# First three projection units made together, their inputs fetched in another order, two warming passes fewer

## The chip, the cores and the metric

The kernel runs on one core of one Trainium2 chip. The metric is the device time of one execution in microseconds (us), taken as the median of several runs. A core has a matrix engine (PE, with PEld as its weight loads), three elementwise engines (DVE, ACT, POOL), and a queue engine (SP) that issues transfers. ACT and POOL can issue transfers as well. Each engine works through its own list of instructions in order and waits on counters (semaphores) that other engines or transfers raise.

## The reference

Two branches over the same input `x` (2048 tokens by 448) are mixed by a gate:

```python
g = sigmoid((x * gate_w).sum(-1, keepdims=True))
q, k, v = split(x @ wqkv)                 # 16 heads of 28
a = softmax(q @ k.T * 28 ** -0.5) @ v     # per head
a = a.reshape(1, 2048, 448) @ wo
gate = x @ W_gate; gate = gate * (gate > 0)
b = (gate * (x @ W_up)) @ W_down          # inner width 1792
out = g * a + (1 - g) * b
```

All inputs and outputs are float32. The kernel keeps that accuracy by cutting operands into two parts: a *high* part, the value rounded to the PE's `float32r` type, and a *low* part, the rest. A product is then the sum of high times high, low times high and high times low.

## The kernel before, in words

The work has three stages: the projections q, k, v and the gate's sums from `x`; attention with the gate and up products mixed in; and the output and down products. Only the start of the first stage changes.

**Tiles.** The 448 rows of `x` and of the weights are cut into four chunks of 128 partitions (the last holds 64 rows twice). The tokens are cut into four blocks of 512 (`tb`). A unit `qk(tb, c)` makes 128 columns of q or k (`c` from 0 to 6) for one block: 11 matmuls of 128x512, listed in `TERMS`, that add up in one PSUM bank. A term `(a, b)` multiplies part `a` of the weights `W` (0 to 2 high of chunks 0 to 2, 3 to 5 their low, 6 the fourth chunk) with part `b` of the tokens `X` (0 to 3 high, 4 to 7 low). Four banks go round for these units.

**Getting the operands.** `load_x(tb)` fetches a block of `x` into staging tiles `xr` (three of them go round, each holds two chunks), `load_w(c)` fetches 224 columns of the weights. `split_first`, `split_x` and `split_w` cut what arrived: `act_high` (line 130, ACT) makes the high part, `low` (line 136, DVE) or `pool_low` (line 139, POOL) subtracts it to make the low one. 224 columns (2*GD) are one group, so unit 0 needs the first group, unit 2 the second, and unit 1 both.

**Order.** The engines' order is the order of the code (a manual schedule). `split_first` takes the first group's four chunks and the tokens' four chunks in this order:

```python
for group in ((weights(0), tokens(0)), (weights(1), tokens(1)), (weights(2), weights(3)),
              (tokens(2), tokens(3))):
```

Then the second group of weights is split (`split_w(*w1)`), and the units follow: (0,0) with its terms by chunk (`BY_CHUNK`), (0,1), (1,0), (1,1), (0,2), (2,0), (2,1), (1,2), (3,0), and from there the list `mixed`, in which units, v products (`vproj`) and the first maxima of the scores (`smax`, line 191) alternate. The scores' maxima begin with unit number 20, counted from the first.

**Before the first unit** PE makes `WARM` passes (line 398): matmuls of zeros, 128x512, whose result is overwritten.

**After a unit** `send()` makes a high and a low copy of its bank (ACT, then DVE), and POOL stores both to DRAM (`qk_d`, line 359). When the four units (0..3, 0) are stored, SP loads from there the K and Q of the first heads (`load_k`, `load_q`, lines 175 and 180).

**Transfers.** Loads are issued by SP (the first two pieces of weights by ACT). Eight counters, DMAHW0 to DMAHW7, are given to these loads in turn: the ninth load has to wait until the first has landed, since it uses the same counter. An `xr` tile can be filled again when DVE has read it.

Of the kernel before, what the change touches and what calls it, by code (L numbers as in the profile page):

```python
# [18 lines left out]
P = 128  # L19
# [17 lines left out]
WARM = 11  # L37
# [41 lines left out]
def gated_mix_kernel(ctx, tc, x, wq, wo, wgu, wd, out):  # L79
# [156 lines left out]
    with tc.tile_pool(name="qkv", bufs=1) as pa:  # L236
        W = pa.tile([P, 7, WC], F32R, name="W")

        def load_w(c):
            c0, c1 = c * 2 * GD, (c + 1) * 2 * GD if c < G + 1 else 2 * D + VC  # L240

            if c in (0, 2, 5):
# [5 lines left out]
            if c > 0:  # L248
                nc.sync.dma_start(wr, wq[:, :, c0:c1])
            return wr, c0, c1  # L250

        def split_w(wr, c0, c1):

            ways = [[(W[:, :, c0:c1], wr)]]
            if c0 < 2 * D:
# [4 lines left out]
                if c0 == 2 * GD:  # L260
                    ways = [[(w[:, :, :, 0], r[:, :, :, 0])], [(w[:, :, a, 1:], r[:, :, a, 1:]) for a in range(2)]]
# [8 lines left out]
        def split_first(wr, xr):  # L270

            r = wr.rearrange("p c (a j d) -> p c a j d", a=2, j=4)
            w = W[:, :, :2 * GD].rearrange("p c (j a d) -> p c a j d", a=2, j=4)

            def weights(c):
                act_high(w[:, c if c < 3 else 6], r[:, c])
                yield

                take = pool_low if c else low
                if c < 3:  # L280
                    take(w[:, 3 + c], r[:, c], w[:, c])
                else:
                    take(w[64:, 6], r[64:, 3], w[64:, 6])
                yield
# [8 lines left out]
            for group in ((weights(0), tokens(0)), (weights(1), tokens(1)), (weights(2), weights(3)),  # L293
                          (tokens(2), tokens(3))):
# [4 lines left out]
        def load_x(tb):  # L299
            r = []  # L300
            for c in range(0, 4, 2):
                xr = pa.tile([P, 2, TB], F32, name=f"xr_{tb}_{c}", tag="stg", bufs=3)
                for a, b in ((c, c + 1), (c + 1, c + 2)) if tb == 0 else ((c, c + 2),):
                    nc.sync.dma_start(xr[:, a - c:b - c], x[:, a:b, tb * TB:(tb + 1) * TB])  # L304
                if tb + c == 0:
                    load_first(nc.sync, 2, 4)
# [42 lines left out]
        def qk(tb, c, terms=TERMS, among=()):  # L349
            ps = ps_any(c == NQ - 1)  # L350
            for n, (a, b) in enumerate(terms):
                nc.tensor.matmul(ps, W[:, a, c * P:(c + 1) * P], xf(tb, b), start=(n == 0), stop=(n == NT - 1))  # L352
                mix(n, among)
            st = st_tile(tb, c)
# [54 lines left out]
        split_first(w0[0], x0)  # L409
# [4 lines left out]
        split_w(*w1)  # L414
        qk(0, 0, BY_CHUNK)
        split_x(1, x1)

# [22 lines left out]
        units = [(qk, 3, 1), (qk, 2, 2), (qk, 3, 2)]  # L440
        units += [(qk, tb, c) for c in range(3, NQ) for tb in range(NB - 1, -1, -1)]
        vs = [(vproj, tb, t) for tb in range(NB - 1, -1, -1) for t in range(4)]
        mixed = units[:2]
# [447 lines left out]
```

## Time and profile before

| what | value |
|---|---|
| median of 3 runs | 1260.32 us (1259.86 to 1260.8) |
| profiled execution: first to last instruction (span) | 1258.2 us |
| median of the runs less that span | 2.1 us |
| PE busy in the span | 1252.8 us of 1258.2 |
| DVE, ACT, POOL busy | 854.8, 748.4, 374.3 us |
| granted PE clock, mean | 1.000 |

The profile shows one execution, and of it only the time from its first to its last instruction; about 2.1 us of a run's time lie outside. A row of the timeline gives a start, a duration, the engine, the line, the operation with its output and input, and in brackets how long the engine was idle before it and what ended that. "us, mean ns" of a group are its total and the mean of one instruction.

### The profile page before, as it was taken

The page shows a single profiled execution, that of the slowest core. Times are in us where ns is not written, and L with a number is a line of the kernel's source. Part 1 is how long each engine was busy: PE and PEld are TensorE (multiplying, and loading weights), DVE is VectorE, ACT ScalarE, POOL GpSimd, SP SyncE. Part 2 cuts the span into 40 slices and gives each one's busy share as a digit, 9 for nine tenths or more (in the row PEclk, how much of TensorE's full clock was granted, in tenths as well). Part 3 has the DMA queues.
Part 4 walks back from the last instruction along what each step waited for, and adds up shares of the span by engine and source line. Part 5 has one row for each costly group of instructions (what it writes and reads, how often), then busy time and mean ns, then how long its engine had stood idle before and what let it go on. Part 6 is the DMA issues. An engine that isn't in the chain of part 4 may idle for free.

```text
span 1258.2 us, 18270 instructions
## 1 busy us (share of the span) xinstructions
PE 1252.8 (100%) x6687; PEld 919.1 (73%) x6687; DVE 854.8 (68%) x1363; ACT 748.4 (59%) x1424; POOL 374.3 (30%) x569
## 2 busy tenths in 40 slices
PE   9999999999999999999999999999999999999998
PEld 6888866677666676666766667766667666899997
DVE  6599767687777797776977778877778224663342
ACT  6312767686666776666866667766677773312121
POOL 4222222312334123423133331134222444651020
PEclk9999999999999999999999999999999999999999
DMA  8955453144245314241544323142431226634432
GB/s 302 315 206 209 117 155 99 50 106 104 60 115 173 81 43 121 68 113 44 130 121 127 100 80 90 43 122 67 114 94 50 84 85 208 223 110 138 145 106 79
DMA packets 54113, 151.00 MB, mean 120 GB/s; under 512 B 10304, under 2 KB 17416, under 8 KB 49160
## 3 DMA queue, kind: packets, MB, share of 16 engines
q1 hardware_dynamic: 36632, 100.44, 29.2%
q0 software_dynamic: 16960, 48.94, 11.0%
q8 instruction: 52, 0.85, 0.3%
q10 hardware_dynamic: 432, 0.46, 0.1%
q14 instruction: 37, 0.30, 0.1%
HBM read 104.16 MB, written 46.03 MB: 119 GB/s over the span
## 4 chain that ended last, share of the span: by engine, by line
PE 99%; DMA 0%; SPq 0%; DVE 0%; ACT 0%; issue 0%
PE b L526 22%; PE b L191 19%; PE b L217 19%; PE b L560 18%; PE b L789 11%; PE b L352 5%; PE b L370 3%; PE b L744 3%; DMA xr<-x 0%; PE b L199 0%; SPq L304 0%; DVE X L136 0%; DVE y L795 0%; ACT X L130 0%; SPq L384 0%
## 5 line engine op out<-in xcount | busy, mean ns | idle before, releaser
L192 DVE TENSOR_REDUCE mx<-b 128x1 f32<-128x512 f32 x1024 | 646.5, 685 | 51.2 <-PE b L191 50.7
L219 ACT ACTIVATE P<-b 128x512 f32<-128x512 f32 x840 | 467.1, 599 | 160.8 <-PE b L217 139.0
L526 PE MATMUL b<-X,wg 128*128 128x512 f32 (+1 forms) x1232 | 415.3, 394 | 0.0
L191 PE MATMUL b<-K,Q 128*128 128x512 f32 x1024 | 389.6, 391 | 0.0
L217 PE MATMUL b<-Q,K 128*128 128x512 f32 x1024 | 389.3, 390 | 0.0
L526 PEld LDWEIGHTS b<-X,wg 128*128 128x128 f32 (+1 forms) x1232 | 220.2, 187 | 53.8 <-issue 9.3
L217 PEld LDWEIGHTS b<-Q,K 128*128 128x128 f32 x1024 | 192.3, 188 | 46.3 <-issue 6.7
L191 PEld LDWEIGHTS b<-K,Q 128*128 128x128 f32 x1024 | 192.4, 188 | 44.3 <-issue 5.9
L560 PE MATMUL b<-P,V 128*32 128x512 f32 x1680 | 188.2, 593 | 0.0
L548 POOL DMA_DIRECT2D h_d<-h x56 | 31.3, 558 | 405.4 <-DVE h L542 354.9
L139 POOL TENSOR_TENSOR wg<-wgr,wg 128x384 fp32r<-128x384 f32 x200 | 143.2, 731 | 10.4 <-DVE wg L133 2.0
L560 PEld LDWEIGHTS b<-P,V 128*32 128x32 f32 x1680 | 52.7, 110 | 120.0 <-issue 116.8
L789 PE MATMUL b<-WD,hh 128*128 128x448 f32 x672 | 138.5, 365 | 0.0
L219 ACT ACTIVATE V<-b 128x512 f32<-128x512 f32 x184 | 105.0, 599 | 48.8 <-PE b L217 42.3
L789 PEld LDWEIGHTS b<-WD,hh 128*128 128x128 f32 x672 | 126.2, 188 | 10.3
L130 ACT ACTIVATE hh<-hr 128x512 fp32r<-128x512 f32 x56 | 35.3, 631 | 124.7 <-PE b L789 120.2
L136 DVE TENSOR_TENSOR hh<-hr,hh 128x512 fp32r<-128x512 f32 x56 | 45.7, 815 | 66.4 <-ACT hh L130 66.3
L352 PE MATMUL b<-X,W 128*128 128x512 f32 x308 | 83.1, 393 | 0.1
L566 DVE TENSOR_TENSOR os<-b,os 128x512 f32<-128x512 f32 x16 | 11.1, 692 | 86.5 <-PE b L560 86.5
L352 PEld LDWEIGHTS b<-X,W 128*128 128x128 f32 x308 | 57.4, 188 | 14.5 <-DVE X L136 1.6
L130 ACT ACTIVATE wg<-wgr 128x384 fp32r<-128x384 f32 x156 | 62.2, 490 | 7.9 <-DMA wgr<-wgu 3.9
L575 POOL DMA_DIRECT2D l_d<-rs x16 | 8.9, 559 | 186.2 <-DVE rs L574 186.2
(74 smaller groups left out, 665.6 us busy)
## 6 DMA issues: line engine op xcount, KB each, us to landing
wgr<-wgu SPq DMA_DIRECT2D x55, 512.0 KB
K<-qk_d SPq DMA_DIRECT2D x64, 224.0 KB
Q<-qk_d SPq DMA_DIRECT2D x64, 224.0 KB
h_d<-h POOLq DMA_DIRECT2D x56, 256.0 KB, 2.7
hr<-h_d SPq DMA_DIRECT2D x56, 256.0 KB
qk_d<-st POOLq DMA_DIRECT2D x21, 512.0 KB, 4.2
x_d<-X POOLq DMA_DIRECT2D x6, 1024.0 KB, 5.4
X<-x_d SPq DMA_DIRECT2D x24, 256.0 KB
```

The costliest lines, as they stand in the source:

```text
L130: nc.scalar.activation(dst, src, AF.Copy)
L136: nc.vector.tensor_tensor(dst, src, f32(high), op=OP.subtract)
L139: nc.gpsimd.tensor_tensor(dst, src, f32(high), op=OP.subtract)
L191: nc.tensor.matmul(ps, Q[h][:, u * P:(u + 1) * P], K[h % 3][:, c * TB:(c + 1) * TB], start=True, stop=True)
L192: nc.vector.tensor_reduce(MX[h][:, 4 * u + c:4 * u + c + 1], ps, axis=AX.X, op=OP.max)
L217: nc.tensor.matmul(ps, K[h % 3][:, kt * P:(kt + 1) * P], Q[h][:, j * TB:(j + 1) * TB], start=True, stop=True)
L219: nc.scalar.activation(PT[i][:, j], ps, AF.Exp, scale=SCALE)
L352: nc.tensor.matmul(ps, W[:, a, c * P:(c + 1) * P], xf(tb, b), start=(n == 0), stop=(n == NT - 1))
L370: nc.tensor.matmul(ps[:, :VC], xf(tb, b)[:, t * P:(t + 1) * P], W[:, a, 2 * D:2 * D + VC], start=(n == 0), stop=(n == NT - 1))
L526: nc.tensor.matmul(ps, WS[i][rows, s, a], xf(i // NF, b)[rows], start=(n == 0), stop=(n == NT - 1))
L560: nc.tensor.matmul(po[32 * j:32 * j + 32], V[:, h // 4 % 2, i % NK, h % 4], p[:, j], start=(i == i0), stop=(i == i0 + ni - 1))
L789: nc.tensor.matmul(ACC[i // NF][t][:, :D], HH[i][:, a, t * P:(t + 1) * P], WD[:, f, b], start=(f == 0 and n == 0), stop=(f == NF - 1 and n ...
```

## The change

- The second group of weights is no longer fetched and split as a whole (`load_w(1)`, `split_w(*w1)` are gone); both groups come chunk by chunk with the tokens, chunk 0 first. The first pieces, chunk 0 of the tokens and chunk 0 of the first group, are fetched in two halves of 64 partitions, one on SP's queue and one on ACT's.
- `split_first` goes by chunk: tokens, first group, second group. For chunk 0 the first group's high part is made by DVE (`dve_high`, line 133). The lows of the first group are made by DVE, those of the second by POOL.
- Units (0,0), (0,1) and (0,2) are made together by `qk_first`: three banks, and for each chunk all terms of all three units, before the next chunk. Their copies and stores come after all 33 matmuls.
- `WARM` is 9 and not 11.
- `split_x(1)` stands ahead of the units. The order of the units is now these three, then (1,0), (1,1), (1,2), (2,0), (2,1), (2,2), (3,0): the fourth block's first unit is the tenth, where it was the ninth. From the twelfth unit on, the order is as before, and the numbers that count units in `mixed` are one lower.

```diff
-WARM = 11
+WARM = 9
...
-            if c in (0, 2, 5):
+            if c == 5:
...
-            if c > 0:
-                nc.sync.dma_start(wr, wq[:, :, c0:c1])
+            nc.sync.dma_start(wr, wq[:, :, c0:c1])
...
-            def weights(c):
-                act_high(w[:, c if c < 3 else 6], r[:, c])
+            def weights(g, c):
+                r = wr[:, c, 2 * GD * g:2 * GD * (g + 1)].rearrange("p (a j d) -> p a j d", a=2, j=4)
+                w = W[:, :, 2 * GD * g:2 * GD * (g + 1)].rearrange("p c (j a d) -> p c a j d", a=2, j=4)
+                (act_high if c + g else dve_high)(w[:, c if c < 3 else 6], r)
                 yield
-                take = pool_low if c else low
+                take = pool_low if g else low
...
-            for group in ((weights(0), tokens(0)), (weights(1), tokens(1)), (weights(2), weights(3)),
-                          (tokens(2), tokens(3))):
+            for c in range(4):
+                group = [tokens(c), weights(0, c), weights(1, c)]
                 for _ in range(2):
...
-                    nc.sync.dma_start(xr[:, a - c:b - c], x[:, a:b, tb * TB:(tb + 1) * TB])
-                if tb + c == 0:
-                    load_first(nc.sync, 2, 4)
+                    if tb + a == 0:
+                        for queue, rows in ((nc.sync, slice(0, 64)), (nc.scalar, slice(64, P))):
+                            queue.dma_start(xr[rows, :1], x[rows, :1, :TB])
+                            load_first(queue, 0, 0, 1, rows)
+                    else:
+                        nc.sync.dma_start(xr[:, a - c:b - c], x[:, a:b, tb * TB:(tb + 1) * TB])
+                    if tb == 0:
+                        load_first(nc.sync, a, a == 0, 2)
...
+        def qk_first():
+            units = [(c, ps_any()) for c in range(3)]
+            for c in range(4):
+                terms = [t for t in TERMS if t[1] % 4 == c]
+                order = [(t, u) for t in terms for u in units]
+                if c == 0:
+                    order = [(terms[n], units[k]) for n, k in ((0, 0), (1, 0), (0, 1), (0, 2), (2, 0), (2, 1), (2, 2), (1, 1), (1, 2))]
+                for (a, b), (u, ps) in order:
+                    nc.tensor.matmul(ps, W[:, a, u * P:(u + 1) * P], xf(0, b), start=b == 0 and a == 0,
+                                     stop=(a, b) == terms[-1] and c == 3)
+            for u, ps in units:
+                send_qk(0, u, ps)
...
+            send_qk(tb, c, ps)
+
+        def send_qk(tb, c, ps):
             st = st_tile(tb, c)
...
-        w0 = load_w(0)
-
-        def load_first(queue, a, b):
-            queue.dma_start(w0[0][:, a:b], wq[:, a:b, w0[1]:w0[2]])
-
-        for c in range(2):
-            load_first(nc.scalar, c, c + 1)
+        def load_first(queue, c, a, b, rows=slice(0, P)):
+            queue.dma_start(w0[rows, c, a * 2 * GD:b * 2 * GD], wq[rows, c, a * 2 * GD:b * 2 * GD])
+
         x0 = load_x(0)
-        w1 = load_w(1)
...
-        split_w(*w1)
-        qk(0, 0, BY_CHUNK)
         split_x(1, x1)
+        qk_first()
...
-        qk(0, 1, HIGH_FIRST)
+        qk(1, 0)
         split_x(2, x2)
         x3 = load_x(3)
-        qk(1, 0)
+        qk(1, 1)
         split_w(*w2)
-        qk(1, 1)
-        qk(0, 2)
+        qk(1, 2)
         split_x(3, x3)
...
-        qk(1, 2)
-        qk(3, 0)
         split_w(*w4)
         w3 = load_w(3)
+        qk(2, 2)
+        qk(3, 0)
```

How the change moves instructions is shown at three places. A row is a line of the code, an operation, its output and input, the output's size, and in brackets the counters that it, or a bare wait standing directly ahead of it, waits for; X_105 is the high part of the first block of tokens, X_106 the low part, V the buffer in which the first weights land. The first place is the head of ACT's list, from its two transfers to the first pieces it splits, before:

```order
L384 DMA V<-wq 128x224 x2
L130 ACT_TABLE_LOAD
L130 ACTIVATE W<-V 128x2x4x28 [waits DMAHW0_49]
L130 ACTIVATE X_105<-xr_0_127 128x512 [waits DMAHW1_49]
L130 ACTIVATE W<-V 128x2x4x28 [waits DMAHW2_49]
L130 ACTIVATE X_105<-xr_0_127 128x512 [waits DMAHW3_49]
```

and with the change, where DMAHW0 counts ACT's half of the first tokens and DMAHW1 SP's half:

```order
L302 DMA xr_0_125<-x 64x512
L402 DMA V<-wq 64x224
L130 ACT_TABLE_LOAD [waits DMAHW1_49]
L130 ACTIVATE X_105<-xr_0_125 128x512 [waits DMAHW0_49]
L130 ACTIVATE W<-V 128x2x4x28 [waits DMAHW4_49]
L130 ACTIVATE X_105<-xr_0_125 128x512 [waits DMAHW5_49]
L130 ACTIVATE W<-V 128x2x4x28 [waits DMAHW6_49]
```

The tokens moved ahead of the weights, and the first ACTIVATE needs two transfers; the wait for one of them is a bare wait that stands ahead of the table load. The second place is PE after its warming passes, before (the first unit alone, bank b_69):

```order
L352 MATMUL b_69<-X_105,W 128x512 [waits Activation_49]
L352 MATMUL b_69<-X_105,W 128x512 [waits DVE_49]
L352 MATMUL b_69<-X_106,W 128x512 [waits DVE_49]
L352 MATMUL b_69<-X_105,W 128x512 [waits Activation_49]
L352 MATMUL b_69<-X_105,W 128x512 [waits Pool_49]
```

and with the change (three banks, b_69, b_70 and b_73):

```order
L366 MATMUL b_69<-X_105,W 128x512 [waits DVE_49,Activation_49]
L366 MATMUL b_69<-X_105,W 128x512 [waits DVE_49]
L366 MATMUL b_70<-X_105,W 128x512 [waits Activation_49]
L366 MATMUL b_73<-X_105,W 128x512
L366 MATMUL b_69<-X_106,W 128x512
L366 MATMUL b_70<-X_106,W 128x512
L366 MATMUL b_73<-X_106,W 128x512
L366 MATMUL b_70<-X_105,W 128x512 [waits Pool_49]
L366 MATMUL b_73<-X_105,W 128x512
```

Chunk 0 now has nine matmuls where it had three; the second in the list still needs DVE, for the low part of the first weights. The third place is DVE between its clearing of the warming operand and the end of the first chunk, before:

```order
L394 MEMSET V 128x256
L136 TENSOR_TENSOR W<-V,W 128x2x4x28 [waits DMAHW0_49,Activation_49]
L136 TENSOR_TENSOR X_106<-xr_0_127,X_105 128x512 [waits DMAHW1_49,Activation_49]
L136 TENSOR_TENSOR X_106<-xr_0_127,X_105 128x512 [waits DMAHW3_49,Activation_49]
L136 TENSOR_TENSOR X_106<-xr_2_131,X_105 128x512 [waits DMAHW5_49,Activation_49]
```

and with the change:

```order
L409 MEMSET V 128x256
L133 CAST W<-V 128x2x4x28 [waits DMAHW3_49,DMAHW2_49]
L136 TENSOR_TENSOR X_106<-xr_0_125,X_105 128x512 [waits DMAHW1_49,DMAHW0_49,Activation_49]
L136 TENSOR_TENSOR W<-V,W 128x2x4x28 [waits DVE_49]
L136 TENSOR_TENSOR X_106<-xr_0_125,X_105 128x512 [waits DMAHW5_49,Activation_49]
```

The copy of the first weights came to DVE, and the low part of these weights, which stood first, now stands behind the low part of the tokens.

More of the change, by code (lines that the diff above doesn't have):

```diff
@@ L447, in gated_mix_kernel @@
             units, vs = units[2:], vs[2:]
-        spills = {15 + 3 * k: (NB - 1 - k // 2, k % 2) for k in range(6)}
-        m, first, ahead = 0, 10, 4 * LEAD + 16
+        spills = {14 + 3 * k: (NB - 1 - k // 2, k % 2) for k in range(6)}
+        m, first, ahead = 0, 9, 4 * LEAD + 16
         for n, (f, *a) in enumerate(mixed):
```

23 lines of the change are left out of this document (10 added, 13 removed).

## The prediction

> **What bounds the kernel now.** I read the page's head first, then the chain that ended last, then busy time by stretch, and only then the first 16 us instruction by instruction.
>
> ```profile
> span 1258.2 us, 18270 instructions
> PE 1252.8 (100%) x6687; PEld 919.1 (73%) x6687; DVE 854.8 (68%) x1363; ACT 748.4 (59%) x1424; POOL 374.3 (30%) x569
> PE 99%; DMA 0%; SPq 0%; DVE 0%; ACT 0%; issue 0%
> 0.00:100.00 100.00, 98.66 (x430) 80.09 (x431) 70.65 (x113) 35.12 (x76) 30.42 (x49) 1.00 0.75 262
> 1200.00:1258.20 58.20, 54.10 (x267) 49.78 (x266) 20.82 (x29) 11.07 (x17) 5.22 (x6) 0.99 0.30 91
> ```
>
> The matrix engine is the bound nearly everywhere: it is on the chain for 99%, idle for 1.34 us in the first 100 us and for 4.10 us in the last 58. The change touches only the start, so what can be had lies there. The chain's first pieces and PE's weight loads show it. In the latter, the bracket names what ended each idle time.
>
> ```profile
> 2.64 4.97 DMA xr<-x
> ...
> 8.30 0.99 DVE X L136
> ...
> 9.33 30.44 PE b L352 x133
> ```
>
> ```profile
> 1.20 4.09 PE L398 MATMUL b<-V 128*128 128x512 bf16 x11 [1.20 <-DVE V L394]
> ...
> 3.73 0.15 PEld L398 LDWEIGHTS <-V 128*128 128x128 bf16 x1 [0.28 <-issue]
> 4.16 0.15 PEld L398 LDWEIGHTS <-V 128*128 128x128 bf16 x1 [0.28 <-issue]
> 4.49 0.31 PEld L398 LDWEIGHTS <-V 128*128 128x128 bf16 x2 [0.17 <-issue]
> 5.37 0.30 PEld L352 LDWEIGHTS b<-X,W 128*128 128x128 f32 x2 [0.57 <-ACT X L130]
> 6.10 0.62 PEld L352 LDWEIGHTS b<-X,W 128*128 128x128 f32 x3 [0.43 <-DVE X L136]
> ...
> 9.33 0.75 PEld L352 LDWEIGHTS b<-X,W 128*128 128x128 f32 x4 [0.36 <-DVE X L136]
> ```
>
> From 9.33 us PE runs without a stop. The 133 matmuls from there take 30.44 us, 0.229 us each, and a unit of 11 takes 2.52. They end with unit 13, 143 matmuls in all, so 10 were done before 9.33. From 5.37 to 9.33 that is 3.96 us for 2.29 us of work: 1.67 us lost while chunks arrive and are split. Between the warming passes, weight loads start 0.43 us apart up to 4.16 and less after it: PE was at about half speed until some 4.3 us, 3.1 us after its first pass.
>
> My yardstick is the end of the 33rd matmul, when units 1 to 3 are done in both kernels. Before: 9.33 + 23 x 0.229 = 14.60 us.
>
> **The change, part by part.** *More work per chunk.* Nine matmuls of chunk 0 are 2.06 us where three were 0.69, more than a chunk takes to split (below). So once chunk 0 is complete, PE no longer waits for the next. That removes the 1.67 us of stalls. What it does to the start depends on the next step.
>
> *The table load.* ACT's first operation needs its table, and the trace has its price:
>
> ```profile
> 1.67 1.28 ACT L130 ACT_TABLE_LOAD   x1 [1.67 <-PEq L884]
> 4.41 0.39 ACT L130 ACTIVATE W<-V 128x224 fp32r<-128x224 f32 x1 [1.46 <-DMA V<-wq]
> 4.71 0.61 ACT L130 ACTIVATE X<-xr 128x512 fp32r<-128x512 f32 x1
> ...
> 4.41 0.39 SPq L304 DMA_DIRECT2D xr<-x  x1
> ...
> 4.83 0.39 DVE L136 TENSOR_TENSOR W<-V,W 128x224 fp32r<-128x224 f32 x1 [3.69 <-ACT W L130]
> 5.35 0.69 DVE L136 TENSOR_TENSOR X<-xr,X 128x512 fp32r<-128x512 f32 x1
> ```
>
> Before, it ran from 1.67 to 2.95, hidden by the wait for data until 4.41. With the change a bare wait for SP's half of the tokens stands ahead of it in ACT's list, so the 1.28 us start when that half lands. No row shows this 128 KB load. The nearest is ACT's first weight piece of 112 KB, issued at the same moment: SP's load that has to wait for its counter goes at 4.41, so it had landed by then. From above, the 256 KB of chunk 0 were there by 4.71. From below, the page's quickest transfer of such size bounds it:
>
> ```profile
> h_d<-h POOLq DMA_DIRECT2D x56, 256.0 KB, 2.7
> L133 DVE CAST wg<-wgr 128x384 fp32r<-128x384 f32 x6 | 1.9, 358 | 0.1
> L139 POOL TENSOR_TENSOR W<-V,W 128x224 fp32r<-128x224 f32 x2 | 1.5, 750 | 3.4 <-ACT W L130 3.4
> L139 POOL TENSOR_TENSOR W<-V,W 64x224 fp32r<-64x224 f32 x1 | 1.1, 1082 | 0.1
> ```
>
> that is 0.75 (the first issue) + 2.7 = 3.45. I take 4.41, the row of the same size and moment. Then: table load to 5.69; high part of the tokens (0.61) to 6.32; PE's first matmul at 6.36, 0.99 later than before; low part of the tokens (DVE, 0.69) to 7.03; low part of the first weights (0.39), now behind it, to 7.42. PE's second matmul waits for that: 7.46. The copy that went to DVE (under 0.36) runs during the table load and costs nothing. From the second matmul, 32 in a row end at 7.46 + 32 x 0.229 = 14.79.
>
> *Is that row unbroken?* ACT needs 0.61 + 2 x 0.39 = 1.39 us per chunk; DVE 0.69 + 0.39 = 1.08; POOL 0.75 to 1.08; PE uses 2.06. ACT reaches the chunks' tokens at 6.7, 8.0 and 9.4, PE needs chunk 1 at 9.3, chunk 2 at 11.4, chunk 3 at 13.4. The loads have about as much cover:
>
> ```profile
> 6.93 1.33 ACT L130 ACTIVATE X<-xr 128x512 fp32r<-128x512 f32 x2
> 8.94 1.42 ACT L130 ACTIVATE W<-wr 128x168 fp32r<-128x168 f32 x6 [0.67 <-DMA wr<-wq]
> ```
>
> Tokens and both weight groups, 1.9 MB, were in by 8.94 before. The bytes are the same, but three of SP's issues (weights 2, tokens 3, weights 3) now wait for counters that come free when the first halves land, so they go after 4.41; even 1.5 us on 8.94 is before ACT's use at 10.4 could hurt PE at 13.4. The block `split_x(1)` follows on ACT at 10.8 and ends, with DVE's lows, near 14.5; unit 4 needs its first high part at 14.8.
>
> *Two warming passes fewer.* The nine end at about 4.7 (the tenth's weights load at 4.49 as the ninth starts). Nothing for PE is ready before 6.36, so this neither gains nor costs, as long as the clock stays up.
>
> *The order of the units* costs PE nothing in itself: units 12 and on follow as before. The fourth block's tokens are needed after nine units and not eight, so this wait gets 2.52 us more room.
>
> *Sum:* 14.79 - 14.60 = +0.19 us on a span of 1258.2. The median of the runs stands 2.1 us above that span, and I put the change on it: 1260.32 + 0.19 = 1260.5. With the landing at 3.45 or 4.71 the sum is -0.77 or +0.49.
>
> **Rivals.** *The clock falls back (slower).* PE now idles from 4.7 to 6.36, does one matmul, and idles until 7.46: 1.66 and 0.87 us of idling within 2.8. For it: the half-speed start above shows that the clock follows activity, and the two spare passes are gone. Against it: stalls of up to 0.57 us in this trace left the pace at 0.229. If it falls back just then, regaining it takes the 3.1 us seen, half of them lost: +0.19 + 1.55 = +1.7; if the regaining is missed once, +0.19 + 3.1 = +3.3. It decides if the stop before the second matmul is long enough. The Trainium skill, "TensorE: Matmul & The Clock Gate" (Part 1, the HAM clock gate) puts the window at about 3.4 us, free-running, and wants one idle window for the fall; by that rule, stops of 1.66 and 0.87 us leave the clock up, and the sum stays as it is. The 3.1 us of slow passes agree with its figure.
>
> *The table load has a tail (slower).* Before, ACT idled 1.46 us behind it and a transfer ended that, so a hidden tail of up to 1.46 us would not have shown. Exposed now, it moves both matmuls: +0.19 + 1.46 = +1.65, and PE would then idle from 4.7 to 7.8 in one piece, which makes the first rival likely on top: +3.2 to +4.8. Against it: the profile shows no instruction there. The Trainium skill, "ScalarE: Activation LUTs" (What ACT_TABLE_LOAD costs) gives 1283 ns, as this trace does, and a drain of about 1380 ns with each switch of tables; by that page the sum would be +1.57. No run here shows a drain.
>
> *The table load goes ahead (faster).* If it runs at 1.67 as before, the high part of the tokens ends at 5.02, both lows at 6.12, and 33 matmuls at 6.15 + 32 x 0.229 = 13.48: -1.1; with data at 3.45, some -2.1. The list of ACT speaks against it.
>
> *The wait goes elsewhere (slower).* The last first-column unit (3,0) is tenth now. Before, its store let head 0's loads go at 38.15; their last was in by 52.76, when SP could reuse its counter; the first maxima needed it at 54.27.
>
> ```profile
> 38.15 1.52 SPq L175 DMA_DIRECT2D K<-qk_d  x2
> ...
> 52.76 0.31 SPq L180 DMA_DIRECT2D Q<-qk_d  x1
> ...
> 54.27 0.39 PE L191 MATMUL b<-K,Q 128*128 128x512 f32 x1
> ...
> 8.79 3.56 POOL L411 MEMSET K<- 32x2048 f32 x2
> ```
>
> That is 1.51 us of room against one unit, 2.52: up to +1.0, and +1.2 with the sum. POOL's clearing of K, 3.56 us, now stands behind its last low part at about 11.7 instead of at 8.79, so the first stores go some 3 us later; if none of that is caught up, about +3. Against it: one store more is then already out of the queues, and fewer bytes stand in front of K and Q. The same room also caps any gain: PE arriving more than 1.5 us early would wait here.
>
> **How the numbers follow.** The sum 0.40; clock 0.18, half of it beyond 2.5 us; tail 0.18, half of it beyond (0.10, since the clock would likely follow); head of ACT's list 0.12; later waits 0.12, half beyond. 0.2% of this time is 2.5 us, about what a measurement of this kernel can tell from no change. Slower by more: 0.09 + 0.10 + 0.06 = 0.25. Faster by more needs over 2.5 us where 1.67 are lost and 1.51 have room: 0.03. Within: 0.72. The range leaves out the best of the fast case and the clock's second miss: 1258.9 to 1263.4, that is -1.4 to +3.1. The likeliest case alone: 1259.5 to 1260.9.
>
> **What would show it.** In the changed profile ACT_TABLE_LOAD starts near 4.4, not at 1.67; PE's first 128x512 of the units comes near 6.4, the second near 7.5, and then no stop until unit 13. If the weight loads of the units start 0.43 us apart after 7.5, the clock fell back; if ACT idles between the table load and its first ACTIVATE, it has a tail; if PE waits near 54 us for Q, head 0 came late. I am wrong if the table load stands at 1.67, or if a chunk's matmuls wait for SP's late issues.

## The result, and the profile after

The changed kernel takes 1263.58 us (median of 21 runs, 1261.15 to 1266.59), the kernel before 1260.36 us on the same chips (21 runs, 1259.78 to 1261.95). The ratio is 1.0024 with a 95% interval of 1.0018 to 1.0031: it is slower by about 3 us, and its runs spread over 5.4 us where those of before spread over 2.2. The profiled execution took 1264.39 us. Its page begins so:

```profile
span 1262.6 us, 18268 instructions
PE 1254.8 (99%) x6685; PEld 921.0 (73%) x6685; DVE 855.2 (68%) x1361; ACT 747.7 (59%) x1421; POOL 374.9 (30%) x570
```

The work is the same, the span 4.4 us longer. By stretch (length, then the busy time of PE, PEld, DVE, ACT and POOL, the granted clock, the share of the DMA engines and GB/s), the idle time of PE in the first 100 us went from 1.34 to 3.68 us; the end of the span shows 3.87 us of it, 0.23 less than before:

```profile
0.00:100.00 100.00, 96.32 (x410) 78.69 (x411) 66.40 (x105) 34.34 (x72) 30.94 (x50) 1.00 0.76 262
1200.00:1262.60 62.60, 58.73 (x290) 54.07 (x288) 21.97 (x31) 13.28 (x20) 6.97 (x6) 1.00 0.30 93
```

The view of what PE waited for names the places. Two are at the start (L366), one at the first maxima (L191), where the K of head 0 comes late, and a small one far behind (L539):

```profile
PE b L191 <- DMA K<-qk_d: 1.2, 1, 1.2
PE b L366 <- DVE W L133: 0.7, 1, 0.7
PE b L366 <- DVE W L136: 0.5, 1, 0.5
PE b L539 <- DVE wg L136: 0.2, 1, 0.2
```

The start in the timeline, on ACT, DVE, PE and POOL:

```profile
1.20 4.02 PE L413 MATMUL b<-V 128*128 128x512 bf16 x9 [1.20 <-DVE V L409]
...
3.62 1.28 ACT L130 ACT_TABLE_LOAD   x1 [3.62 <-DMA xr<-x]
...
4.91 0.63 ACT L130 ACTIVATE X<-xr 128x512 fp32r<-128x512 f32 x1
...
5.52 0.28 DVE L133 CAST W<-V 128x224 fp32r<-128x224 f32 x1 [4.38 <-DMA V<-wq]
5.71 0.68 DVE L136 TENSOR_TENSOR X<-xr,X 128x512 fp32r<-128x512 f32 x1
...
5.94 0.77 PE L366 MATMUL b<-X,W 128*128 128x512 f32 x1 [0.73 <-DVE W L133]
...
6.21 0.71 POOL L139 TENSOR_TENSOR W<-V,W 128x224 fp32r<-128x224 f32 x1 [3.52 <-ACT W L130]
...
6.31 0.85 DVE L136 TENSOR_TENSOR W<-V,W 128x224 fp32r<-128x224 f32 x1
...
7.22 10.27 PE L366 MATMUL b<-X,W 128*128 128x512 f32 x32 [0.51 <-DVE W L136]
```

The table load stands behind the landing of the tokens, as forecast, and the second matmul comes at 7.22. The low part of the first weights, for which it waits, took 0.85 us here and 0.39 before. But the 32 matmuls from there take 10.27 us and not 7.33. In stretches of 2.5 us (length, PE's busy time with the matmuls in it, granted clock, DMA share, GB/s) PE is busy without a break and yet makes 7 matmuls where 11 fit:

```profile
7.50:10.00 2.50, 2.50 (x7) 1.00 1.03 381
10.00:12.50 2.50, 2.50 (x7) 1.00 0.71 245
12.50:15.00 2.50, 2.50 (x11) 1.00 0.57 207
```

That is half speed until about 13.2 us, though the clock's column says 1.00. The yardstick, the end of the 33rd matmul, is 17.49, against 14.60 before.

The second place in the chain of waits (start, duration, what): the store of unit (3,0), the first load of K that it lets go, and the first maxima.

```profile
38.17 5.46 DMA qk_d<-K
43.64 0.02 SPq L175
43.71 0.41 SPq L175
...
58.34 0.47 PE b L191
```

Before, K went at 38.15 and the first maxima stand at 54.44 in the chain. Now it is 43.71 (+5.56) and 58.34 (+3.90). These 3.90 us and the 0.23 at L539 make up 4.1 of the span's 4.4 us; for the rest I found no single place.

How the 3.90 come about in this execution can be counted. PE reaches the maxima 17.49 - 14.60 = 2.89 us late. K and Q are late by this and by one unit more ahead of (3,0), 2.52: 5.41 of the measured 5.56. The room was 1.51, so PE should wait 5.41 - 2.89 - 1.51 = 1.0 us; the trace says 1.2. What the execution does not tell is whether the slow start or the late K is the cause of the 3 us: each hides part of the other. That was for the experiments to tell.

### The profile page after: what moved, and what is told of

It is laid out like the page before. It is cut to its first block, busy times and chain, and to the rows that moved or that the text cites. A ratio compares the mean times of both kernels' runs of the same rounds, so it can differ in the third digit from the quotient of the medians.

```text
span 1262.6 us, 18268 instructions
## 1 busy us (share of the span) xinstructions
PE 1254.8 (99%) x6685; PEld 921.0 (73%) x6685; DVE 855.2 (68%) x1361; ACT 747.7 (59%) x1421; POOL 374.9 (30%) x570
## 4 chain that ended last, share of the span: by engine, by line
PE 96%; DMA 2%; DVE 1%; issue 0%; ACT 0%; POOL 0%; ACTq 0%; SPq 0%; DVEq 0%; POOLq 0%
PE b L539 22%; PE b L191 19%; PE b L217 19%; PE b L573 18%; PE b L802 11%; PE b L757 3%; PE b L353 3%; PE b L388 2%; DMA K<-qk_d 1%; PE b L366 1%; DMA xr<-x 1%; DMA qk_d<-K 0%; DMA V<-wq 0%; PE b L199 0%; DVE wg L136 0%
## 5 line engine op out<-in xcount | busy, mean ns | idle before, releaser
L539 PE MATMUL b<-X,wg 128*128 128x512 f32 (+1 forms) x1232 | 415.5, 394 | 0.2 <-DVE wg L136 0.2
L191 PE MATMUL b<-K,Q 128*128 128x512 f32 x1024 | 389.7, 391 | 1.2 <-DMA K<-qk_d 1.2
L539 PEld LDWEIGHTS b<-X,wg 128*128 128x128 f32 (+1 forms) x1232 | 220.1, 187 | 54.4 <-issue 9.3
L191 PEld LDWEIGHTS b<-K,Q 128*128 128x128 f32 x1024 | 192.3, 188 | 45.9 <-issue 7.5
L353 PE MATMUL b<-X,W 128*128 128x512 f32 x275 | 73.8, 390 | 0.0
L577 DVE COPY os<-b 128x512 f32<-128x512 f32 x16 | 11.1, 691 | 77.2 <-PE b L573 77.2
```

Source lines behind the costliest of these rows:

```text
L191: nc.tensor.matmul(ps, Q[h][:, u * P:(u + 1) * P], K[h % 3][:, c * TB:(c + 1) * TB], start=True, stop=True)
L539: nc.tensor.matmul(ps, WS[i][rows, s, a], xf(i // NF, b)[rows], start=(n == 0), stop=(n == NT - 1))
```

## The experiments

Theory 1: the slow first matmuls (the clock) are the loss. Theory 2: the loss is the wait for K and Q of head 0, and what happens ahead of it hardly matters. Theory 3: the table load and the order of DVE's first pieces are the loss. Each ratio is to the kernel before on the same chip, whose medians were 1260.11 to 1260.19 us.

This table has the profiled execution of each (us): the second matmul, the row of 32 from there, the end of the 33rd, when the first load of K goes, PE's wait for K or Q, the start of the first maxima in the chain, what was lost by half speed right behind it, and the span.

| kernel | 2nd | row of 32 | 33rd | K goes | wait | first maxima | half speed | span |
|---|---|---|---|---|---|---|---|---|
| before | | | 14.60 | 38.15 | 0 | 54.44 | 0 | 1258.2 |
| after | 7.22 | 10.27 | 17.49 | 43.71 | 1.2 | 58.34 | 0 | 1262.6 |
| e1: 15 passes | 7.14 | 7.55 | 14.69 | 42.02 | 2.9 | 57.17 | 0 | 1261.0 |
| e2: order of units | 6.79 | 7.55 | 14.34 | 39.82 | 0 | 55.72 | 0 | 1259.3 |
| e3: table load first | 6.94 | 9.17 | 16.11 | 42.93 | 2.8 | 58.54 | 1.7 | 1263.9 |
| e5: third block sooner | 7.17 | 10.45 | 17.62 | 41.68 | 0 | 57.22 | 0 | 1260.8 |
| e6: before, order of after | | | | 40.09 | 2.0 | 56.44 | 1.7 | 1262.1 |
| e7: e2 and e5 | 6.76 | 7.57 | 14.33 | 41.16 | 0.8 | 56.28 | 0 | 1260.1 |
| e8: e7, passes, POOL | 7.84 | 7.55 | 15.39 | 39.39 | 1.4 | 56.37 | 0 | 1260.7 |
| e9: maxima a unit later | 7.64 | 10.30 | 17.94 | 44.19 | 0.5 | 60.59 | 0 | 1262.0 |
| e10: whole first loads | 6.22 | 9.45 | 15.67 | 41.07 | 1.8 | 57.12 | 1.7 | 1262.6 |
| e11: e7, old buffer | 7.59 | 9.16 | 16.75 | 41.02 | 0 | 56.36 | 0 | 1260.3 |
| e12: e10 and e11 | 6.26 | 7.55 | 13.81 | 39.47 | 3.0 | 56.61 | 0 | 1260.5 |

In every row the span less that of before is the shift of the first maxima plus the half speed behind it, within 0.6 us (e9's maxima stand 2.52 us later by its edit). Whatever the changed start gains or loses is settled there: by PE's arrival or by K's and Q's, whichever is later.

**e1: more warming passes.** The changed kernel with 15.

```diff
-WARM = 9
+WARM = 15
```

> The changed kernel with 15 warming passes and not 9; nothing else differs. Theory 1 (clock): in the changed kernel PE stopped from 5.2 to 5.9 and again to 7.2 us, and its first 14 or so unit matmuls then stood 0.43 us apart, which cost 2.9 us at the 33rd matmul. Six more passes fill the stop, so the unit matmuls stand 0.23 us apart from the start, the 33rd ends near 14.7 and not at 17.5, and the median falls from 1263.6 to about 1261.4 (what is left being the wait for head 0's K near 54 us, some 1.2 us). Theory 2 (that wait alone, the slow start being made up before it): time unchanged at 1263.6, since K's loads set the pace.

Measured: 1265.70 us (6 runs, 1261.33 to 1266.99), ratio 1.0037 [1.0024, 1.0049]. The profile shows the clock's part mended, in the chain:

```profile
7.14 7.55 PE b L366 x32
...
57.17 0.47 PE b L191
```

The 33rd matmul ends at 14.69, 2.8 us sooner than in the changed kernel, and the maxima start only 1.2 us sooner, since PE now waits 2.9 us there:

```profile
PE b L191 <- DMA K<-qk_d: 2.9, 1, 2.9
```

The median is no better. So the slow start alone is not the cause of the time: with it gone, the wait takes its place. The clock has a part in it all the same. The profiled execution and one other have a mean granted clock of 1.000 and took 1262.74 and 1261.33 us; the other four, at 0.999 or 0.997, took 1265.42 to 1266.99. The timeline of ACT shows a further delay of K that the slow start had mostly covered:

```profile
33.07 1.04 ACT L130 ACTIVATE W<-wr 128x672 fp32r<-128x672 f32 x2 [2.50 <-DMA wr<-wq]
34.02 1.07 ACT L130 ACTIVATE K<-b 128x512 fp32r<-128x512 f32 x2
```

PE was done with (3,0) at about 14.69 + 7 x 2.51 = 32.3. Its copy, the second of these two, starts 2.2 us after that, because the split of the weights `w4` stands ahead of it and ACT waited 2.50 us for their load. In the changed kernel itself the same rows are

```profile
34.35 1.05 ACT L130 ACTIVATE W<-wr 128x672 fp32r<-128x672 f32 x2 [1.72 <-DMA wr<-wq]
35.30 1.06 ACT L130 ACTIVATE K<-b 128x512 fp32r<-128x512 f32 x2
```

and PE was done at about 17.49 + 7 x 2.51 = 35.1, so there the copy, at about 35.8, was only some 0.7 us late. In the kernel before it was the other way round:

```profile
29.83 0.60 ACT L130 ACTIVATE K<-b 128x512 fp32r<-128x512 f32 x1 [1.37 <-PE b L352]
30.73 1.05 ACT L130 ACTIVATE W<-wr 128x672 fp32r<-128x672 f32 x2 [0.30 <-DMA wr<-wq]
```

**e4: nine passes in the kernel before.**

```diff
-WARM = 11
+WARM = 9
```

> The kernel before with 9 warming passes and not 11; nothing else differs. PE's stop ahead of its first unit matmul at 5.4 grows from under 0.1 to 0.2 to 0.7 us. Theory 1 in its strict form (any shortfall of passes keeps the clock down): weight loads of the units 0.43 us apart for some us, median up by 1 to 3 us. In its weak form (only the long stops of the changed kernel matter): median within 0.4 us of 1260.4.

Measured: 1260.15 us (11 runs), ratio 1.0000 [0.9991, 1.0009]. Two passes fewer cost nothing by themselves. There PE goes from its passes, which end at 5.19, straight to the first matmul at 5.20; in the changed kernel it has two stops there, of 0.7 and 0.5 us.

**e3: the table load ahead.** An ACTIVATE of one column, without a wait, as ACT's first work, so that the table is loaded early; what it writes is overwritten later.

```diff
+        act_high(zt[:, :1], V[:, 3, 0, 0, :1])
```

> The changed kernel with one ACTIVATE of 128x1 ahead of ACT's first wait, so that the table load runs at about 2.2 and not behind the landing of the tokens. By the prediction's step (the table load's 1.28 us is on the path of the second unit matmul) that matmul comes 1.1 to 1.3 us earlier, near 6.0, and the median falls by about as much. By the trace of the changed kernel the first weights landed only at 5.5 and DVE's copy of them stands ahead of the low parts, so the second matmul comes 0.2 us earlier at most and the time stays within 0.5 us of 1263.6.

Measured: 1264.92 us (5 runs), ratio 1.0036 [1.0024, 1.0048]. With the table load off the path (it runs from 2.26), the second matmul comes at 6.94, 0.28 sooner, and by just these 0.28 us DVE could start sooner on the first weights (5.24 against 5.52), whose copy and two low parts still stand between. So the table load itself was worth nothing here, and theory 3 falls as far as the table load goes. The order of DVE's first pieces was not tested by itself; that e10 below gains 1.0 us at the second matmul and nothing in the median speaks against it. This execution also lost time by half speed at two places; here the clock's column shows it (1 us each: PE's busy time, matmuls, granted clock, DMA share, GB/s):

```profile
6.00:7.00 1.00, 0.20 (x2) 1.00 0.87 283
7.00:8.00 1.00, 1.00 (x4) 0.78 0.99 330
8.00:9.00 1.00, 1.00 (x4) 0.50 0.91 327
```

**e2: the old place of the fourth block's unit.** Unit (3,0) ninth again, unit (2,2) behind it; the split of `w4` stays ahead of it, where the change put it.

```diff
-        qk(2, 2)
         qk(3, 0)
...
-        units = [(qk, 3, 1), (qk, 3, 2)]
+        units = [(qk, 3, 1), (qk, 2, 2), (qk, 3, 2)]
...
-        m, first, ahead = 0, 9, 4 * LEAD + 16
+        m, first, ahead = 0, 10, 4 * LEAD + 16
```

> The changed kernel with the fourth block's first unit (3,0) in its old place, ninth, and (2,2) behind (3,1); start, transfers and 9 passes as in the change. Theory 2: head 0's loads are let go one unit (2.5 us) earlier than at 43.7, PE does not wait for K, and the median falls by the 1.2 us of that wait, to 1262.4. Theory 1: the slow start stays, the 33rd matmul still ends near 17.5, and what remains over the kernel before is 2 us or more. If the fourth block's tokens are late (they landed at 30.6 with the change), PE waits for them instead, up to 2 us: then no gain or a loss.

Measured: 1261.54 us (11 runs, 1261.06 to 1263.02), ratio 1.0013 [1.0004, 1.0021]: the excess over the kernel before falls from 3.2 to 1.35 us, so 1.9 us are gone with this one edit, and so is most of the spread. The wait for K is gone from the profile, and PE waits instead for the fourth block's tokens:

```profile
PE b L353 <- ACT X L130: 1.3, 1, 1.3
PE b L366 <- DVE W L133: 0.8, 1, 0.8
PE b L366 <- DVE W L136: 0.3, 1, 0.3
```

Those 1.3 us are the new shift of the maxima (55.72 - 54.44). This speaks for theory 2.

**e6: the new order alone, in the kernel before.** The lines of e2 the other way round, and the split of `w4` ahead of both units, as in the changed kernel.

```diff
-        qk(3, 0)
         split_w(*w4)
         w3 = load_w(3)
+        qk(2, 2)
+        qk(3, 0)
```

> The kernel before with (2,2) ahead of (3,0), so that (3,0) is the tenth unit; nothing of the start is changed. Theory 2b: head 0's loads go one unit later than at 38.15, K and Q are in near 55.2 instead of 52.8, PE waits about 1 us, and the median rises to 1261.2 to 1261.5. Theory 2a: a store more is out of the way by then, so K and Q are in by 54.3 and the median stays within 0.3 us of 1260.2.

Measured: median 1260.47 us, ratio 1.0008 [0.9999, 1.0017]. The median hides two outcomes: eight runs lie from 1260.02 to 1260.87, three from 1263.88 to 1264.15. The profiled execution is one of the three, and shows what such a run is. PE waits, and then goes on at half speed:

```profile
PE b L191 <- DMA Q<-qk_d: 2.0, 1, 2.0
```

```profile
56.00:57.00 1.00, 0.56 (x3) 1.00 0.92 320
57.00:58.00 1.00, 1.00 (x5) 0.75 0.90 287
58.00:59.00 1.00, 1.00 (x4) 0.50 0.97 348
59.00:60.00 1.00, 1.00 (x4) 0.50 0.86 262
60.00:61.00 1.00, 1.00 (x4) 0.54 1.00 315
61.00:62.00 1.00, 1.00 (x5) 1.00 0.84 295
```

From 57 to 61 us the granted clock adds up to 0.25 + 0.50 + 0.50 + 0.46 = 1.7 us lost. With the wait of 2.0 that is 3.7, which is how far the three runs lie from the others. So a wait for K or Q costs its own length, and if the clock falls behind it, 1.7 us on top. The split of `w4` is not what made Q late here, since ACT was done with it before PE had finished (3,0):

```profile
32.31 0.60 ACT L130 ACTIVATE K<-b 128x512 fp32r<-128x512 f32 x1 [0.88 <-PE b L352]
```

The new order of the units is enough to bring an execution there. But in eight of the eleven runs it cost nothing that can be told from noise, so with the old start the order alone does not make 3 us.

**e9: the first maxima one unit later.** The changed kernel with one unit more between the loads of K and their first use.

```diff
-        m, first, ahead = 0, 9, 4 * LEAD + 16
+        m, first, ahead = 0, 10, 4 * LEAD + 16
```

> The changed kernel with the first maxima one unit later (from the 21st unit, not the 20th, the same number of them in the units that are left); all else as in the change. Theory 2 (what the change loses is lost where the first maxima wait for head 0's K and Q, which land at 57 to 58.5): PE has one unit, 2.5 us, more to do before it needs them, so the wait shrinks from 1.2 to 2.9 us to under 1, and the median falls from 1263.6 by 1 to 2.5 us, to 1261 to 1262.5. Theory 1 (the slow first matmuls cost the time): no change. A loss of its own is possible where DVE has more maxima per unit to reduce.

Measured: 1262.32 us (11 runs), ratio 1.0016 [1.0007, 1.0025]: the excess over the kernel before is 2.2 us where it was 3.2, by nothing but room. The wait in the profile falls from 1.2 to 0.5, not to 0, since K went 0.5 us later and took longer. Theory 2 stands again.

**e5: the third block's split sooner.** The change had also put `split_x(2)` behind unit (1,0), 44 matmuls from the start where it was 22; its end frees the tile into which half of the fourth block's tokens are loaded (they land at 30.59 in the changed kernel, 25.94 before).

```diff
-        qk(1, 0)
         split_x(2, x2)
+        qk(1, 0)
```

> The changed kernel with the third block's split (split_x(2)) ahead of unit (1,0)'s copy on ACT and DVE and not behind it; PE's order, the tenth place of (3,0) and the start are as in the change. Theory 2a (chain of the late K: X2's split stands behind the copy of the fourth unit, so the staging tile comes free at 22.8 and not at 16, the fourth block's tokens land at 28.5 to 30.6, and ACT's copies behind them let the store of (3,0) go at 37 to 38): the last tokens are issued near 17 to 18 and land by 26.5, the store of (3,0) goes near 33.5, K and Q of head 0 are in near 54, PE waits 0 to 1 us there, and the median falls to 1260.5 to 1261.5. Theory 2b (the tenth place of (3,0) alone makes K late): the wait of about 1.2 to 2.9 us stays, and with it 1263 or more.

Measured: 1263.25 us (10 runs, 1262.46 to 1269.65), ratio 1.0030 [1.0019, 1.0040]. The tokens land at 27.3 and the wait for K is gone in the profile, where PE itself comes late through the slow clock (33rd at 17.62). The maxima start 2.8 us later than before, about as late as the 33rd matmul ends (3.0 us). The median hardly moves. So in this execution, where K was in time, it is the slow start that is paid: to mend K's side alone brings as little as to mend the clock's side alone did in e1.

**e10: the first loads whole.** The first weights on ACT's queue, the first tokens on SP's, instead of halves of both on each.

```diff
-                        for queue, rows in ((nc.sync, slice(0, 64)), (nc.scalar, slice(64, P))):
-                            queue.dma_start(xr[rows, :1], x[rows, :1, :TB])
-                            load_first(queue, 0, 0, 1, rows)
+                        load_first(nc.scalar, 0, 0, 1)
+                        nc.sync.dma_start(xr[:, :1], x[:, :1, :TB])
```

> The changed kernel with the first pieces fetched as before: the first weights whole on ACT's queue, the first tokens whole on SP's, not in halves on both. With the halves, the first weights landed at 5.2 to 5.5 and the second unit matmul came at 6.8 to 7.2. Now the weights should land near 4.4 and the tokens by 4.7, with the table load run before; the second unit matmul comes near 6.4, 0.4 to 0.8 us earlier. Theory 2: this gain is lost at the wait for head 0's K and Q, and the median stays within 0.7 us of 1263.6. Theory 1: the shorter stop of PE brings the clock up in more runs, and the median falls by 1 us or more.

Measured: 1264.41 us (6 runs), ratio 1.0034 [1.0021, 1.0046]. The second matmul comes 1.0 us sooner, and the wait eats it. PE and its wait:

```profile
6.22 9.45 PE L365 MATMUL b<-X,W 128*128 128x512 f32 x32 [0.57 <-DVE W L136]
```

```profile
PE b L191 <- DMA Q<-qk_d: 1.8, 1, 1.8
PE b L365 <- DVE W L136: 0.6, 1, 0.6
```

and the clock falls behind it as in e6, from 58 to 61.5 us:

```profile
57.00:58.00 1.00, 0.88 (x4) 1.00 0.99 287
58.00:59.00 1.00, 1.00 (x4) 0.53 1.06 373
59.00:60.00 1.00, 1.00 (x4) 0.50 0.89 254
60.00:61.00 1.00, 1.00 (x4) 0.50 0.92 266
61.00:62.00 1.00, 1.00 (x5) 0.77 0.89 311
```

**e7 and e8: parts together.** e7 is e2 with e5's edit. e8 adds 15 passes and puts POOL's clearing of K ahead of its first low parts:

```diff
-        split_first(w0, x0)
         for k in K[:2]:
             nc.gpsimd.memset(f32(k)[96:128], -1.0)
+        split_first(w0, x0)
```

> The changed kernel with both: (3,0) in its old ninth place and the third block's split ahead of unit (1,0)'s copy. In the run with the old order alone PE waited 1.3 us for the fourth block's tokens, which landed at 27.9. Theory 2a: they land by 26.5 now, neither wait is left, and what remains is the start: the 33rd matmul at 14.3 to 14.7 with a warm clock, at 17.5 with a cold one, where it was 14.6 before. So the median comes to 1260.0 to 1260.6 if the clock is mostly up, and to 1261.5 to 1263 if it is mostly not.

> As the run before, and with 15 warming passes, and POOL's clearing of the rows of K ahead of its first low parts and not behind them, so that the first stores go about 3 us earlier. Theory 1 and 2 together: the clock is up at the first unit matmul, no wait for tokens or K is left, the 33rd matmul ends near 14.5, and the median is 1260.0 to 1260.3, no more than 0.3 us from the kernel before. If the median stays above 1261, a wait is left that neither theory names.

Measured: e7 1261.87 us (11 runs), ratio 1.0014 [1.0005, 1.0022]; e8 1262.49 us (11 runs), 1.0020 [1.0011, 1.0029]. Neither is better than e2. In e7 K goes at 41.16 although PE runs as early as before, and in e8 at 39.39, but head 0 is in only at about 56.2, 16.8 us later, where it took 14.6 before. In e7 the copy of (3,0) starts at 34.92, some 5.5 us after PE was done with it (14.33 + 6 x 2.51 = 29.4), behind the split of `w4`, whose load came in at 33.9; in e8 it starts 2.3 us after. That K goes sooner does not bring head 0 in as much sooner: in the profiles where PE waited at the maxima, K goes between 39.39 and 43.71 (leaving out e9), a spread of 4.3 us, and the maxima start between 56.28 and 58.54, a spread of 2.3.

In e8 the earlier clearing had a price of its own: POOL was at it from 2.75 to 6.29, and DVE's copy of the first weights, 0.28 us in the other runs, took 1.61 us beside it. The second matmul came at 7.84, the latest of all.

**e11 and e12: the old buffer for the third weights, and all that helped.** The change lets the third group of weights use the tile `wr`, so that the load of `w4`, which needs it, waits for their split (issued at 25.91 in the changed kernel, 16.43 before). e11 is e7 with these weights in their old place:

```diff
-            if c == 5:
+            if c in (2, 5):
```

> The changed kernel with three parts of the later loads undone: (3,0) ninth again, the third block's split ahead of unit (1,0)'s copy, and the third group of weights in its old buffer (V) so that the fourth group's load need not wait for its split. The start (units by chunk, halves on two queues, 9 passes) stays. Theory 2: the fourth group of weights is issued near 18 and not at 23 to 26, DMA is as full from 20 to 40 us as before, K and Q of head 0 are in by 54.5, and the median is 1260.0 to 1261.0, what is left being the clock in some runs. If K and Q still land at 56, the halved and reordered first loads themselves are behind it.

e12 is e11 with e10's queues.

> As the run before, with the first pieces fetched as before (weights on ACT's queue, tokens on SP's). Theory 2 and the earlier start together: the second unit matmul near 6.4, the 33rd near 13.9 with the clock up, no wait behind; the median 1259.7 to 1260.3, the best that these parts can do. If the median is above 1260.8, the order of the first three units itself costs.

Measured: e11 1262.07 us (11 runs), ratio 1.0015 [1.0007, 1.0024]; e12 1260.86 us (12 runs, 1259.25 to 1265.20), ratio 1.0009 [1.0001, 1.0017]. e12 is the best of the changed start. Its 33rd matmul ends 0.8 us before that of the kernel before, and two of its runs are below any run of that. Still the median isn't: it lies just above the 1260.8 from which on the expectation blamed the order of the first three units. The profile of e12 shows something else. PE waits 3.0 us for K, and ACT shows a part of why:

```profile
PE b L191 <- DMA K<-qk_d: 3.0, 1, 3.0
```

```profile
31.95 1.04 ACT L130 ACTIVATE W<-wr 128x672 fp32r<-128x672 f32 x2 [3.39 <-DMA wr<-wq]
32.90 0.58 ACT L130 ACTIVATE K<-b 128x512 fp32r<-128x512 f32 x1
```

PE ended (3,0), ninth here, at about 13.81 + 6 x 2.51 = 28.9. Its copy runs at 32.90, 4.0 us later, behind the split of `w4`, whose load had been issued at 17.66 and was in at 31.9. So the earlier load didn't help; what holds the copy is the split's place ahead of it, which the change brought and which all runs from e1 to e12 on the changed start have in common. But the copy is not the whole wait. Its store landed 4.4 us after its issue (35.05 to 39.45) where the one before took 6.7 (31.45 to 38.15), so K went only 1.3 us later than before. The 3.0 us add up from this 1.3, from 2.5 that head 0's load took longer (17.1 us, not 14.6) and from 0.7 that PE came sooner, less the room of 1.5. The longer load is the largest part.

**What stays open.** The one edit that follows from this, the split of `w4` (and the load `w3`) behind unit (3,0) again, was not run; that it would give back a part is an inference from the rows of e1 and e12, and by the sum for e12 it would not be all. Nor is it settled why the 1.8 MB of head 0 take 14.6 us in some executions and up to 17.1 in others. From 45 to 57 us the DMA engines were busy for 0.87 to 1.02 of the time in the profiles of before, after, e1, e3, e6, e7, e8, e10 and e12, so that what else they had to move may set when K and Q are in; no run tested this. No version that was run beats the kernel before in the median.

## Where the prediction was right and where it was wrong

The forecast of next to no change, 1260.5, was wrong: the change is slower by 3 us. The range's upper end, 1263.4, is close to what came: 1260.32 x 1.0024 = 1263.3, while the median of the 21 runs is 0.2 us above it. That it reached so far is in part luck: its upper part stood there for the clock falling back, for a tail of the table load and for POOL's clearing of K, none of which came as told. One of the rivals, *the wait goes elsewhere*, names the place where the time was lost; it had a chance of 0.12.

**The step that failed** is *the order of the units costs PE nothing in itself*: the sum put the later K and Q at nothing. In its place the runs show the wait at the first maxima. The rival's working, one unit of 2.52 against 1.51 of room, holds in the profiled execution (1.0 counted, 1.2 measured), and e2 shows that taking the unit back recovers 1.9 of the 3.2 us. But the price of that rival, +1.0 to +1.2, was too small, and four things were missing from it:

- The diff moved `split_w(*w4)` ahead of (3,0), and so put a wait for a load ahead of the copies that K and Q hang on: some 0.7 us in the changed kernel's profile, 2.2 in e1, 4.0 in e12. The prediction spoke of the buffers' later issues only at the start, not of the weights `w4` at all.
- The load of head 0 was taken to last as long as before, 14.6 us. It took up to 17.1 (e12).
- Behind a wait of some 2 us the clock can fall, 1.7 us more (e3, e6, e10).
- The unit's later place was taken to be partly made up for by emptier queues ("one store more is then already out of the queues"). No row showed K and Q landing sooner for it, and they did not.

The rival's other branch, about +3 because POOL's clearing of K would hold up the stores, did not come: ahead of the two stores of which the second is that of (3,0), POOL had stood idle for 2.19 us, waiting for DVE.

```profile
37.45 1.45 POOL L377 DMA_DIRECT2D qk_d<-K  x2 [2.19 <-DVE K L136]
```

The order is not the cause by itself either: with the old start (e6) it cost nothing in eight of eleven runs. And the later place did serve the fourth block's tokens, as forecast: with the unit ninth (e2) PE waits 1.3 us for them, about all of the 1.35 us that are left there. e7 has the tokens sooner, and in its profile waits for K again. Which mix of these waits makes the 3 us in the median run stays open.

**More work per chunk** did what it was forecast to do: from the second matmul to the first maxima PE has no stop in the changed profile, and the 1.67 us of stalls between chunks are gone.

**The table load** stands where it was forecast (3.62 to 4.90; the landing taken was 4.41, bounds 3.45 to 4.71), and without a tail: its ACTIVATE starts 0.01 us behind it. The Trainium skill, "ScalarE: Activation LUTs" (What ACT_TABLE_LOAD costs), gives 1283 ns, which the 1.28 here bear out, and a drain of about 1380 ns with a switch of tables, which this first load doesn't show. The working from there came close by errors that cancelled. *The copy costs nothing* failed, since the first weights landed at 5.5 and not by 4.7, so that the copy and both low parts came one after the other on DVE; and the low part of these weights took 0.85 us and not 0.39. But the tokens landed 0.8 us sooner than taken, and so the second matmul came at 7.22 where 7.46 was forecast. That this is so near is luck. Nor was the table load on the path any more: in e3, without it, the start is sooner only by as much as the weights are.

**Two warming passes fewer** cost nothing in the kernel before (e4), as forecast. In the changed kernel the forecast's condition, *as long as the clock stays up*, didn't hold: in the profiled execution it had not come up when the passes ended at 5.22, and the matmuls ran at half speed until 13.2. That the stops behind the passes put it off is likely, but not shown, since e2, e7 and e12 started fast with the same nine passes and such stops. This is close to the clock's rival, in its size too (+2.9 at the 33rd matmul; +1.7 to +3.3 was given for the total), though there the clock was to fall back and here it had not come up. Its price does not add to that of the wait, as the later of the two sides counts: e1 took the slow start away and paid the wait instead, and e5 had no wait and paid the slow start.

**The same room caps any gain**, the last sentence of that rival, was right: the 1.0 us that e10 gained at the start were lost at the wait.

## What to carry to other kernels

Before pricing an edit at a kernel's start, find the next place where PE joins with a transfer and write down how much room it has; here it was 1.5 us. Work out both sides, the engine's arrival and the transfer's, since the later one counts and to mend one alone may gain nothing. Then follow back what that transfer hangs on (the load, the store that releases it, the copies in front of the store) and look at each list for what the edit moved ahead of them: a split that waits for a load, in front of a copy that others wait for, can turn a harmless late load into a stop of the bound engine. Do not take the transfer's length as fixed, either. Judge by the spread too: an edit that uses up the room shows first in some runs, not in the median.

## What the runs showed of the hardware that was not expected

**The clock falls behind shorter stops than thought, and not always.** In the profiled executions it fell to half for about 3.4 us behind waits of 1.8 (e10), 2.0 (e6) and 2.8 us (e3); behind waits of 2.9 (e1) and 3.0 (e12) it did not. At the start, with the same nine passes and stops of at most 1.0 us each around the first matmul, the row of 32 took 7.55 us in some profiled executions (e2, e12; 7.57 in e7), 9.16 and 9.17 in others (e11, e3), where the clock was up for the first matmul and fell again, and 9.45 to 10.45 in a third kind (e10, the changed kernel, e9, e5), where it had not come up. The Trainium skill, "TensorE: Matmul & The Clock Gate" (Part 1, the HAM clock gate), describes a free-running window of about 3.4 us and a count of slow matmuls that differs from run to run. The spell of about 3.4 us and the three kinds of start agree with that. Its condition for the fall, at least one idle window, does not fit a fall behind a wait of 1.8 us.

**The clock's column doesn't show a start that was never fast.** In the changed kernel four matmuls per us ran at "1.00" up to 13 us; e3, with four per us as well, shows 0.50. In both the pace of the matmuls tells the truth. Over whole runs the mean granted clock of the kernel before was 0.999 or 1.000 in each of 84 runs of these comparisons; in nine of the 21 of the changed kernel it was 0.997 or 0.998. These nine took 1264.1 us in the median, the other twelve 1262.6, so falls of the clock are a part of the 3 us, and not all of it.

**A transfer cut in two by rows was not in sooner.** The first weights as halves on both queues, behind the tokens' halves, were there for DVE at 4.77 to 5.56 in the profiles of the changed start; as one load at the head of ACT's queue, in e10 and e12, at 4.22 and 4.27. Place and cut changed together here, so which of the two made them late is not shown. For the tokens, first in the queue either way, the cut alone can be read: both halves were in by 4.05 (e3), the whole in e10 by 4.04.

**DVE's subtraction took twice as long where POOL's had begun first.** The low part of the first weights on DVE took 0.85 us where POOL's first low part had begun 0.10 to 0.28 us ahead of it (the changed kernel, e1, e3, e5, e9, e10, e11, e12), and 0.38 or 0.39 where DVE began first (e2 by 0.11, e7 by 0.01). In e8, beside POOL's clearing, DVE's copy took 1.61 us where it took 0.28 elsewhere.
